# Second expert's first two token blocks interleaved, its weights decoded there instead of parked in DRAM

## Chip, core and metric

The kernel runs on one core of a Trainium2 chip. The metric is the device time of one execution in microseconds, as the median of several runs. TensorE does the matrix multiplications (PE, with PEld for its weight loads), VectorE (DVE), ScalarE (ACT) and GpSimd (POOL) the elementwise work, and SyncE's queue (SP) issues the transfers.

## What is computed

Three stages follow one another. A complex gated linear recurrence over 768 time steps for 4 batches of 8 heads of dimension 48 gives a matrix x of 3072 tokens by 384. Two feed-forward experts are applied to all tokens:

```
x  = attention(q, k, v, a_re, a_im)               # 3072 x 384
x1 = (sigmoid(x @ w_gate) * (x @ w_val)) @ w_out  # 384 -> 1536 -> 384
h  = x1 @ w2_in                                   # 384 -> 2048
out = (h * sigmoid(h)) @ w2_out                   # 2048 -> 384
```

The weights of the experts are held as float64 in DRAM.

## The kernel before

**Layout and stages.** Tokens are cut into 24 chunks of 128. The recurrence treats one chunk after another as a pipeline of small functions (s_load_a, s_nat1, s_den1, s_mix1 and so on); a list of "beats" says which function of which chunk is emitted when. The first expert treats nine blocks of chunks, three with two chunks and six with three (256 and 384 tokens). Each block has F1 = 12 steps, one for 128 hidden columns: 9 matmuls for the gate, 9 for the value, and 9 for the output of the step before. The recurrence's beats are spread among the steps of the blocks up to block 7. The second expert treats eight blocks (NB2) of 384 tokens in F2 = 16 steps each: 9 matmuls for h into ps_h, and 9 for the output of the step before into three accumulators acc.

**Split operands.** A product in full precision is three fast matmuls (mm3, L402 to L405): each operand is a high part and a remainder. The chain behind a step's matmuls in the second expert is: Tanh on ScalarE (L974), (tanh + 1) * h on VectorE into sg (L976), the high part hh on ScalarE (L980), the remainder hl on VectorE (L982). In the first expert the same four are L896, L899, L907, L909. TensorE needs hh and hl one step later.

**Weights.** A weight is one tile of 128 x 384 values. w_load (L326) brings its 64-bit words, 384 KB, by SP's queue. w_decode (L344) makes a float32 of them: L348 on ScalarE, L349 and L350 on VectorE, L351 on GpSimd. w_split (L354) makes the high part on ScalarE (L357) and the remainder (L358) on GpSimd and VectorE by turns. conv_to (L747) brings an expert's weights in order up to a given number; it loads up to four and decodes up to two weights ahead. The first expert's 36 weights stay in the 37 slots of the pool wpool, and each slot becomes free behind its last use in block 8. The pool w2p, with twelve slots, opens when the recurrence is over (close_att, L818).

**The second expert's 32 weights.** The first twelve (ND, direct=12) are decoded by conv_to (L926) in the first expert's last two blocks, once the recurrence's beats are out: from step 8 of block 7 on, the count of steps times rate2/10 = 1.8, at most 8 in block 7 (w2slots minus l2). The other twenty are *parked*: from block 2, step 6 on, every third step decodes and splits one weight (park, L371; its load by park_load, L365) and writes the result, 384 KB, to DRAM (w2_d, L378). The split there is L376 on ScalarE and L377 on VectorE. In block 8 unpark_to (L381) reads them back into freed slots of wpool (L385).

**Second expert.** Block by block, step by step (L959 to L993). The next block's input is loaded at step 2 (x1_load, L795) and split at step 13 (x1_split, L800: L803 on ScalarE, L804 on VectorE). Accumulators come from the pools pot and pacc by turns. finish2 (L947) writes a block's result. From block 1 on, check_to (L832) loads every one of the 68 weights again and checks its range (w_guard, L331: L338 on VectorE, L342 on ScalarE), eight weights in ten steps, tied behind the step's own instructions.

**What sets the order.** TensorE runs its instructions in program order (man=['PE']). The other engines' instructions and the transfers are put into order at build time by a scheduler that works with the program's order as priority and a model of the times. At run time each engine and each queue is strictly in order.

Of the kernel before, what the change touches and what calls it, by code (L numbers as in the profile page):

```python
# [9 lines left out]
F32 = mybir.dt.float32  # L10
F32R = mybir.dt.float32r
# [29 lines left out]
    gr=8,  # L41
# [36 lines left out]
    wrate=80,  # L78
    wlead=12,
    w2slots=12,  # L80
    rate2=18,
    c2a=16,
    rate3=20,
    park=30,
    direct=12,
    pacc=8,
    ve='GV',
    beats=8,
# [161 lines left out]
def tile_kernel(ctx, tc, q, k, v, a_re, a_im, w_gate, w_val, w_out, w2_in, w2_out, out):  # L250
# [93 lines left out]
    def w_decode(raw):  # L344
        lo, hi = raw[:, :, :, 0], raw[:, :, :, 1]
        two = wst.tile([128, 2, KD, 128], I32, tag="two", name="two")
        tmp, rnd = two[:, 0], two[:, 1]
        A.activation(rnd, lo.bitcast(U32), AF.Copy, scale=2.0 ** -29)  # L348
        V.tensor_scalar(tmp, hi, 3, 0x3FFFFFFF, ALU.logical_shift_left, ALU.bitwise_and)  # L349
        V.scalar_tensor_tensor(hi, hi, -0x40000000, tmp, ALU.bitwise_and, ALU.bitwise_or)  # L350
        G.tensor_tensor(hi, hi, rnd, ALU.add)  # L351
        return raw, two

    def w_split(pool, raw, nm, n):  # L354
# [2 lines left out]
        A.copy(t[:, 0], w)  # L357
        (V if CFG["ve"][n % len(CFG["ve"])] == "V" else G).tensor_tensor(t[:, 1], w, t[:, 0].bitcast(F32), ALU.subtract)  # L358
        return t

    w2_d = [dram.tile([128, 2, KD, 128], F32, name=f"w2_d{n}") for n in range(2 * F2)]
    ND = CFG["direct"]
    parked = [ND, None]

    def park_load():  # L365
        n = parked[0]
        raw = wst.tile([128, KD, 128, 2], I32, tag="two", name="raw2")
        src2(*order2[n])(raw)
        parked[1] = raw

    def park():  # L371
        n = parked[0]
        raw, two = w_decode(parked[1])
        w = raw[:, :, :, 1].bitcast(F32)
        two = two.bitcast(F32R)
        A.copy(two[:, 0], w)  # L376
        V.tensor_tensor(two[:, 1], w, two[:, 0].bitcast(F32), ALU.subtract)  # L377
        SP.dma_start(w2_d[n], two.bitcast(F32))  # L378
        parked[0] += 1

    def unpark_to(n):  # L381
        while unparked[0] < min(n, 2 * F2):
            i = unparked[0]
            t = wpool.tile([128, 2, KD, 128], F32R, tag="w", name="w2")
            SP.dma_start(t.bitcast(F32), w2_d[i])  # L385
            w2[order2[i]] = t
            unparked[0] += 1

    unparked = [ND]

    EA = 32
    EB = D - EA
# [402 lines left out]
    def x1_load(i):  # L795
        xs = w2p.tile([128, KD, BT2], F32, tag="xs", name="xs", bufs=3)
        SP.dma_start(xs, x1_d[:, :, i * BT2:(i + 1) * BT2].rearrange("k p t -> p k t"))
        return xs
# [13 lines left out]
    def src2(f, j):  # L812
        return (w_in_src(w2_in, f), w_out_src(w2_out, f))[j]
# [9 lines left out]
            pot = fast.enter_context(tc.tile_pool(name="pot", bufs=3, space=PSUM))  # L823

    w2p = pot = None
    c2f = psteps = 0
    conv2 = dict(ld=0, dec=0, sp=0)
    with tc.manual_schedule(engines={getattr(mybir.EngineType, e) for e in CFG["man"]}):
        checks = [src1(*o) for o in order1] + [src2(*o) for o in order2]
# [22 lines left out]
        for gi, group in enumerate(groups):  # L852
# [23 lines left out]
            for si, (i, f) in enumerate(steps):  # L876
                n = blocks[i] * C
                col = sum(blocks[b] for b in group if b < i) * C
                conv_to(conv1, order1, src1, pool1, w1, 3 * (f + 1))
                if f == 0:  # L880
                    beats_upto(0, beats_for(i))
                psg = pgv.tile([128, BT], F32, tag="g", name="ps_g")
                psv = pgv.tile([128, BT], F32, tag="v", name="ps_v")
                for ps, j in ((psg, 0), (psv, 1)):
                    for kk in range(KD):
                        if i == 0:
                            PE.matmul(ps[:, :n], word(f, j, kk), xT[i][0][:, kk, :n], start=kk == 0, stop=kk == KD - 1)
                            continue
                        w = w1[f, j]
                        xh, xl = xT[i]  # L890
                        mm3(ps[:, :n], w[:, 0, kk], w[:, 1, kk], xh[:, kk, :n], xl[:, kk, :n], kk == 0, kk == KD - 1)
                    if ps is psg:
                        sg = hp.tile([128, BT], F32, tag="sg", name="sg")
                        need(ATAN, SIN)
                        with crit():
                            lut(A.activation(sg[:, :n], psg[:, :n], AF.Tanh, scale=0.5))  # L896
                        beats_upto(2 * si + 1)
                with crit():
                    V.scalar_tensor_tensor(sg[:, :n], sg[:, :n], 1.0, psv[:, :n], ALU.add, ALU.mult)  # L899
                if prev is not None:  # L900
                    moe_out(*prev)
                if i == 0:
                    h = (sg,)
                else:
                    h = (hp.tile([128, BT], F32R, tag="hh", name="hh"), hp.tile([128, BT], F32R, tag="hl", name="hl"))
                    with crit():
                        A.copy(h[0][:, :n], sg[:, :n])  # L907
                    with crit():
                        V.tensor_tensor(h[1][:, :n], sg[:, :n], h[0][:, :n].bitcast(F32), ALU.subtract)  # L909
                if si == 0 and gi:  # L910
                    finish1(*fin)
                conv_to(conv1, order1, src1, pool1, w1, 3 * (f + 1) + CFG["wlead"])
                if 12 * i + f >= CFG["park"] and parked[0] < 2 * F2:
                    psteps += 1
                    if psteps % 3 == 0:
                        park()
                        if parked[0] < 2 * F2:
                            park_load()
                    elif psteps == 1:
                        park_load()  # L920
                if done == nbeats and i >= NB - 2:
                    assert parked[0] == 2 * F2
                    close_att()
                    c2f += 1
                    lim2 = len(order2) if i == NB - 1 else CFG["w2slots"] - CFG["l2"]
                    conv_to(conv2, order2[:ND], src2, pool2, w2, min(c2f * CFG["rate2"] // 10, lim2))  # L926
                    if i == NB - 1:
                        unpark_to(ND + 2 * (f - 1))
                beats_upto(2 * si + 2)
                if i == NB - 1 and f == 2:  # L930
                    raw_n = x1_load(0)
                if i == NB - 1 and f == 7:
                    nxt = x1_split(raw_n)
                prev = (f, h, [a[:, col:col + n] for a in acc], n,
                        si == 0, si == len(steps) - 1)
# [20 lines left out]

        NB2 = NT // BT2
        prev = None
        for i in range(NB2):  # L959
            cur = nxt  # L960
            acc = [(pacc if i % 2 else pot).tile([128, 512], F32, tag="acc", name="acc2") for _ in range(BT2 // 128)]
            for f in range(F2):
                conv_to(conv2, order2[:ND], src2, pool2, w2, ND)
                unpark_to(2 * (f + 1))
                if f == 2 and i + 1 < NB2:
                    raw_n = x1_load(i + 1)
                ps = pgv.tile([128, BT], F32, tag="gv"[f % 2], name="ps_h")
                w = w2[f, 0]
                for kk in range(KD):
                    mm3(ps[:, :BT2], w[:, 0, kk], w[:, 1, kk], cur[0][:, kk], cur[1][:, kk], kk == 0, kk == KD - 1)  # L970
                sg = hp.tile([128, BT], F32, tag="sg", name="sg2")
                need(ATAN, SIN)
                with crit():
                    lut(A.activation(sg[:, :BT2], ps[:, :BT2], AF.Tanh, scale=0.5))  # L974
                with crit():
                    V.scalar_tensor_tensor(sg[:, :BT2], sg[:, :BT2], 1.0, ps[:, :BT2], ALU.add, ALU.mult)  # L976
                hh = hp.tile([128, BT], F32R, tag="hh", name="hh2")
                hl = hp.tile([128, BT], F32R, tag="hl", name="hl2")
                with crit():
                    step["A"] = A.copy(hh[:, :BT2], sg[:, :BT2])  # L980
                with crit():
                    step["V"] = V.tensor_tensor(hl[:, :BT2], sg[:, :BT2], hh[:, :BT2].bitcast(F32), ALU.subtract)  # L982
                if prev is not None:
                    moe2_out(*prev)
                    if prev[0] == F2 - 1:
                        finish2(i - 1, prev[2])
                if f == F2 - 3 and i + 1 < NB2:
                    nxt = x1_split(raw_n)
                unpark_to(2 * F2)
                if i:  # L990
                    gs += 1
                    check_to(gs * CFG["gr"] // 10)
                prev = (f, (hh, hl), acc)  # L993
        assert checked == len(checks)
        moe2_out(*prev)
        finish2(NB2 - 1, prev[2])
    bad = lim[:, 4:8]
    good = const.tile([1, 1], I32, name="good")
    V.tensor_reduce(bad[:, 0:1], under, AX.X, ALU.add)
# [43 lines left out]
```

## Time and profile before

| | |
|---|---|
| median of 3 runs | 1155.65 us (1153.68 to 1159.09) |
| profiled execution, own time | 1156.26 us |
| its span, first to last instruction | 1154.5 us |
| TensorE (PE) busy in the span | 1070.1 us, 93% |
| VectorE (DVE) busy | 737.9 us, 64% |
| ScalarE (ACT) busy | 647.3 us, 56% |
| GpSimd (POOL) busy | 251.7 us, 22% |
| HBM read, written | 89.65 MB, 17.30 MB |

All times in the profile are microseconds from the span's start unless marked ns. A wait is put down to the instruction that released it. A group of instructions bears the line of the kernel (L349) that issued it; a helper's line stands for all its callers. A matmul's shown duration overlaps the next one's, so the distance of two starts is the better measure of what one takes. The granted clock of TensorE is 1.00 of full speed from 100 us on.

### The profile page before, as it was taken

How to read it: one execution, taken by the hardware profiler on the slowest of the kernel's cores; microseconds unless marked ns; L12 is line 12 of the kernel's file. 1: busy time of each engine (PE TensorE's matmuls, PEld its weight loads, DVE VectorE, ACT ScalarE, POOL GpSimd, SP SyncE). 2: the span in 40 equal slices, each digit the busy share in tenths (PEclk: the TensorE clock that was granted, in tenths of full speed). 3: DMA queues.
4: the chain of work that ended last, by engine and by line, in shares of the span. 5: the costliest groups of instructions: out<-in, count | busy, mean ns of one | idle time of the engine just before them, and what ended most of it. 6: DMA issues, size and time to landing. Idle time of an engine off the chain costs nothing.

```text
span 1154.5 us, 20813 instructions
## 1 busy us (share of the span) xinstructions
PE 1070.1 (93%) x7786; PEld 1036.1 (90%) x7786; DVE 737.9 (64%) x1336; ACT 647.3 (56%) x1270; POOL 251.7 (22%) x253
## 2 busy tenths in 40 slices
PE   0568989999999999999999999999999999999998
PEld 0457878999999999999999989999999999999997
DVE  7889987788777877776676393334454555545333
ACT  6685877778776666666663252234444454545332
POOL 6566653223333322222221060000000000000000
PEclk9978999999999999999999999999999999999999
DMA  9574445463555554423222349701343443400000
GB/s 241 125 222 131 119 101 152 122 157 94 134 128 129 142 130 115 93 63 83 63 50 66 95 136 302 244 1 55 104 137 96 151 137 96 130 1 21 1 22 23
DMA packets 222522, 127.33 MB, mean 110 GB/s; under 512 B 132944, under 2 KB 210128, under 8 KB 222416
## 3 DMA queue, kind: packets, MB, share of 16 engines
q1 hardware_dynamic: 222416, 125.94, 40.2%
q8 instruction: 63, 1.03, 0.4%
q14 instruction: 43, 0.35, 0.1%
HBM read 89.65 MB, written 17.30 MB: 93 GB/s over the span
## 4 chain that ended last, share of the span: by engine, by line
PE 61%; DVE 14%; DMA 9%; ACT 6%; issue 4%; SPq 4%; POOL 2%; DVEq 0%; POOLq 0%; ACTq 0%
PE acc L405 8%; PE acc L404 8%; PE acc L403 8%; PE ps_h L405 5%; PE ps_h L404 5%; PE ps_h L403 5%; PE ps_v L403 3%; PE ps_g L403 2%; PE ps_g L405 2%; PE ps_g L404 2%; PE ps_v L405 2%; PE ps_v L404 2%; PE ps_a L610 2%; DMA raw<-in_moe_w_out_dram 2%; DVE two L349 2%
## 5 line engine op out<-in xcount | busy, mean ns | idle before, releaser
L976 DVE SCALAR_TENSOR_TENSOR sg<-sg,ps_h 128x384 f32<-128x384 f32 x128 | 70.7, 553 | 133.3 <-ACT sg L974 133.3
L974 ACT ACTIVATE sg<-ps_h 128x384 f32<-128x384 f32 x128 | 62.9, 492 | 147.9 <-PE ps_h L405 147.9
L405 PE MATMUL acc<-w,hl 128*128 128x384 f32 x384 | 129.2, 336 | 2.7 <-DVE hl L982 2.5
L403 PE MATMUL acc<-w,hh 128*128 128x384 f32 x384 | 128.9, 336 | 0.4 <-ACT hh L980 0.2
L404 PE MATMUL acc<-w,hh 128*128 128x384 f32 x384 | 128.4, 334 | 0.0
L405 PE MATMUL ps_h<-xh,w 128*128 128x384 f32 x384 | 128.3, 334 | 0.0
L403 PE MATMUL ps_h<-xh,w 128*128 128x384 f32 x384 | 128.3, 334 | 0.0
L404 PE MATMUL ps_h<-xl,w 128*128 128x384 f32 x384 | 128.3, 334 | 0.0
L982 DVE TENSOR_TENSOR hl<-sg,hh 128x384 fp32r<-128x384 f32 x128 | 71.3, 557 | 66.7 <-ACT hh L980 66.7
L980 ACT CAST hh<-sg 128x384 fp32r<-128x384 f32 x128 | 65.8, 514 | 74.2 <-DVE sg L976 74.0
L403 PE MATMUL ps_v<-xh,w 128*128 128x384 f32 (+1 forms) x288 | 97.4, 338 | 6.6 <-DVE sg L899 6.6
L351 POOL TENSOR_TENSOR raw<-raw,two 128x384 int32<-128x384 int32 x68 | 77.5, 1140 | 118.2 <-DVE raw L350 47.4
L907 ACT CAST hh<-sg 128x384 fp32r<-128x384 f32 (+1 forms) x96 | 46.5, 484 | 100.7 <-DVE sg L899 100.7
L899 DVE SCALAR_TENSOR_TENSOR sg<-sg,ps_v 128x384 f32<-128x384 f32 (+1 forms) x108 | 54.0, 500 | 71.1 <-PE ps_v L405 70.4
L404 PE MATMUL acc<-hl,w 128*128 128x384 f32 (+1 forms) x288 | 94.2, 327 | 5.1 <-DVE hl L909 5.0
L403 PE MATMUL ps_g<-xh,w 128*128 128x384 f32 (+1 forms) x288 | 96.3, 334 | 1.5 <-ACT sg L896 1.5
L403 PE MATMUL acc<-hh,w 128*128 128x384 f32 (+1 forms) x288 | 92.8, 322 | 0.1
L405 PE MATMUL acc<-hh,w 128*128 128x384 f32 (+1 forms) x288 | 92.6, 322 | 0.0
L404 PE MATMUL ps_v<-xl,w 128*128 128x384 f32 (+1 forms) x288 | 92.6, 321 | 0.0
L405 PE MATMUL ps_g<-xh,w 128*128 128x384 f32 (+1 forms) x288 | 92.6, 321 | 0.0
L405 PE MATMUL ps_v<-xh,w 128*128 128x384 f32 (+1 forms) x288 | 92.5, 321 | 0.0
L404 PE MATMUL ps_g<-xl,w 128*128 128x384 f32 (+1 forms) x288 | 92.5, 321 | 0.0
(151 smaller groups left out, 2915.6 us busy)
## 6 DMA issues: line engine op xcount, KB each, us to landing
raw<-in_moe_w_out_dram SPq DMA_DIRECT2D x56, 384.0 KB, 3.8
raw<-in_moe_w_in_dram SPq DMA_DIRECT2D x32, 384.0 KB, 3.5
raw<-in_moe_w_gate_dram SPq DMA_DIRECT2D x24, 384.0 KB, 3.9
raw<-in_moe_w_val_dram SPq DMA_DIRECT2D x24, 384.0 KB, 4.1
w_d<-two SPq DMA_DIRECT2D x20, 384.0 KB, 3.7
w<-w_d SPq DMA_DIRECT2D x20, 384.0 KB, 4.4
kst<-kc SPq DMA_DIRECT2D x72, 64.5 KB, 2.7
kst<-r SPq DMA_DIRECT2D x72, 64.5 KB, 2.8
```

Of the source, the lines that this page charges most:

```text
L349: V.tensor_scalar(tmp, hi, 3, 0x3FFFFFFF, ALU.logical_shift_left, ALU.bitwise_and)
L351: G.tensor_tensor(hi, hi, rnd, ALU.add)
L403: PE.matmul(o, lhi, rhi, start=first, stop=False)
L404: PE.matmul(o, lhi, rlo, start=False, stop=False)
L405: PE.matmul(o, llo, rhi, start=False, stop=last)
L610: PE.matmul(ps[:, h, :], kst[:, g * hh + h, 1:CX], qst[:, g * hh + h, :], start=True, stop=True)
L899: V.scalar_tensor_tensor(sg[:, :n], sg[:, :n], 1.0, psv[:, :n], ALU.add, ALU.mult)
L907: A.copy(h[0][:, :n], sg[:, :n])
L974: lut(A.activation(sg[:, :BT2], ps[:, :BT2], AF.Tanh, scale=0.5))
L976: V.scalar_tensor_tensor(sg[:, :BT2], sg[:, :BT2], 1.0, ps[:, :BT2], ALU.add, ALU.mult)
L980: step["A"] = A.copy(hh[:, :BT2], sg[:, :BT2])
L982: step["V"] = V.tensor_tensor(hl[:, :BT2], sg[:, :BT2], hh[:, :BT2].bitcast(F32), ALU.subtract)
```

## The change

Parking is gone: w2_d, park_load, park and unpark_to, with their calls. All 32 weights of the second expert go through conv_to: rate2 falls from 18 to 12, so the 16 steps at the end of the first expert bring 19 of them, and the second expert's steps go on with one a step (c2a + n2, to 32 at the sixteenth step). The first two blocks of the second expert run together: steps of block 0 and block 1 alternate, block 1 two steps behind (lag=2), so that each weight is used by both blocks soon after it is decoded. Block 1's input is loaded at the first step and split ahead of block 1's first. The banks of ps_h alternate by the running number of the step. The checks begin with block 2.

```diff
@@ -78,11 +78,10 @@
     wrate=80,
     wlead=12,
     w2slots=12,
-    rate2=18,
+    rate2=12,
     c2a=16,
     rate3=20,
-    park=30,
-    direct=12,
+    lag=2,
     pacc=8,
     ve='GV',
     beats=8,
@@ -358,36 +357,6 @@
         (V if CFG["ve"][n % len(CFG["ve"])] == "V" else G).tensor_tensor(t[:, 1], w, t[:, 0].bitcast(F32), ALU.subtract)
         return t
 
-    w2_d = [dram.tile([128, 2, KD, 128], F32, name=f"w2_d{n}") for n in range(2 * F2)]
-    ND = CFG["direct"]
-    parked = [ND, None]
-
-    def park_load():
-        n = parked[0]
-        raw = wst.tile([128, KD, 128, 2], I32, tag="two", name="raw2")
-        src2(*order2[n])(raw)
-        parked[1] = raw
-
-    def park():
-        n = parked[0]
-        raw, two = w_decode(parked[1])
-        w = raw[:, :, :, 1].bitcast(F32)
-        two = two.bitcast(F32R)
-        A.copy(two[:, 0], w)
-        V.tensor_tensor(two[:, 1], w, two[:, 0].bitcast(F32), ALU.subtract)
-        SP.dma_start(w2_d[n], two.bitcast(F32))
-        parked[0] += 1
-
-    def unpark_to(n):
-        while unparked[0] < min(n, 2 * F2):
-            i = unparked[0]
-            t = wpool.tile([128, 2, KD, 128], F32R, tag="w", name="w2")
-            SP.dma_start(t.bitcast(F32), w2_d[i])
-            w2[order2[i]] = t
-            unparked[0] += 1
-
-    unparked = [ND]
-
     EA = 32
     EB = D - EA
 
@@ -823,7 +792,7 @@
             pot = fast.enter_context(tc.tile_pool(name="pot", bufs=3, space=PSUM))
 
     w2p = pot = None
-    c2f = psteps = 0
+    c2f = 0
     conv2 = dict(ld=0, dec=0, sp=0)
     with tc.manual_schedule(engines={getattr(mybir.EngineType, e) for e in CFG["man"]}):
         checks = [src1(*o) for o in order1] + [src2(*o) for o in order2]
@@ -910,22 +879,11 @@
                 if si == 0 and gi:
                     finish1(*fin)
                 conv_to(conv1, order1, src1, pool1, w1, 3 * (f + 1) + CFG["wlead"])
-                if 12 * i + f >= CFG["park"] and parked[0] < 2 * F2:
-                    psteps += 1
-                    if psteps % 3 == 0:
-                        park()
-                        if parked[0] < 2 * F2:
-                            park_load()
-                    elif psteps == 1:
-                        park_load()
                 if done == nbeats and i >= NB - 2:
-                    assert parked[0] == 2 * F2
                     close_att()
                     c2f += 1
                     lim2 = len(order2) if i == NB - 1 else CFG["w2slots"] - CFG["l2"]
-                    conv_to(conv2, order2[:ND], src2, pool2, w2, min(c2f * CFG["rate2"] // 10, lim2))
-                    if i == NB - 1:
-                        unpark_to(ND + 2 * (f - 1))
+                    conv_to(conv2, order2, src2, pool2, w2, min(c2f * CFG["rate2"] // 10, lim2))
                 beats_upto(2 * si + 2)
                 if i == NB - 1 and f == 2:
                     raw_n = x1_load(0)
@@ -956,44 +914,56 @@
 
         NB2 = NT // BT2
         prev = None
-        for i in range(NB2):
-            cur = nxt
-            acc = [(pacc if i % 2 else pot).tile([128, 512], F32, tag="acc", name="acc2") for _ in range(BT2 // 128)]
-            for f in range(F2):
-                conv_to(conv2, order2[:ND], src2, pool2, w2, ND)
-                unpark_to(2 * (f + 1))
-                if f == 2 and i + 1 < NB2:
-                    raw_n = x1_load(i + 1)
-                ps = pgv.tile([128, BT], F32, tag="gv"[f % 2], name="ps_h")
-                w = w2[f, 0]
-                for kk in range(KD):
-                    mm3(ps[:, :BT2], w[:, 0, kk], w[:, 1, kk], cur[0][:, kk], cur[1][:, kk], kk == 0, kk == KD - 1)
-                sg = hp.tile([128, BT], F32, tag="sg", name="sg2")
-                need(ATAN, SIN)
-                with crit():
-                    lut(A.activation(sg[:, :BT2], ps[:, :BT2], AF.Tanh, scale=0.5))
-                with crit():
-                    V.scalar_tensor_tensor(sg[:, :BT2], sg[:, :BT2], 1.0, ps[:, :BT2], ALU.add, ALU.mult)
-                hh = hp.tile([128, BT], F32R, tag="hh", name="hh2")
-                hl = hp.tile([128, BT], F32R, tag="hl", name="hl2")
-                with crit():
-                    step["A"] = A.copy(hh[:, :BT2], sg[:, :BT2])
-                with crit():
-                    step["V"] = V.tensor_tensor(hl[:, :BT2], sg[:, :BT2], hh[:, :BT2].bitcast(F32), ALU.subtract)
-                if prev is not None:
-                    moe2_out(*prev)
-                    if prev[0] == F2 - 1:
-                        finish2(i - 1, prev[2])
-                if f == F2 - 3 and i + 1 < NB2:
-                    nxt = x1_split(raw_n)
-                unpark_to(2 * F2)
-                if i:
-                    gs += 1
-                    check_to(gs * CFG["gr"] // 10)
-                prev = (f, (hh, hl), acc)
+        lag = CFG["lag"]
+        steps2 = []
+        for f in range(F2 + lag):
+            steps2 += [(0, f)] if f < F2 else []
+            steps2 += [(1, f - lag)] if f >= lag else []
+        steps2 += [(i, f) for i in range(2, NB2) for f in range(F2)]
+        xs_n, x2, accs = {}, {0: nxt}, {}
+        n2 = 0
+        for i, f in steps2:
+            n2 += 1
+            if f == 0:
+                accs[i] = [(pacc if i % 2 else pot).tile([128, 512], F32, tag="acc", name="acc2") for _ in range(BT2 // 128)]
+                if i == 0:
+                    xs_n[1] = x1_load(1)
+                elif i == 1:
+                    x2[1] = x1_split(xs_n.pop(1))
+            cur = x2[i]
+            conv_to(conv2, order2, src2, pool2, w2, 2 * (f + 1))
+            if f == 2 and i and i + 1 < NB2:
+                xs_n[i + 1] = x1_load(i + 1)
+            ps = pgv.tile([128, BT], F32, tag="gv"[n2 % 2], name="ps_h")
+            w = w2[f, 0]
+            for kk in range(KD):
+                mm3(ps[:, :BT2], w[:, 0, kk], w[:, 1, kk], cur[0][:, kk], cur[1][:, kk], kk == 0, kk == KD - 1)
+            sg = hp.tile([128, BT], F32, tag="sg", name="sg2")
+            need(ATAN, SIN)
+            with crit():
+                lut(A.activation(sg[:, :BT2], ps[:, :BT2], AF.Tanh, scale=0.5))
+            with crit():
+                V.scalar_tensor_tensor(sg[:, :BT2], sg[:, :BT2], 1.0, ps[:, :BT2], ALU.add, ALU.mult)
+            hh = hp.tile([128, BT], F32R, tag="hh", name="hh2")
+            hl = hp.tile([128, BT], F32R, tag="hl", name="hl2")
+            with crit():
+                step["A"] = A.copy(hh[:, :BT2], sg[:, :BT2])
+            with crit():
+                step["V"] = V.tensor_tensor(hl[:, :BT2], sg[:, :BT2], hh[:, :BT2].bitcast(F32), ALU.subtract)
+            if prev is not None:
+                moe2_out(prev[1], *prev[2:])
+                if prev[1] == F2 - 1:
+                    finish2(prev[0], prev[3])
+            if f == F2 - 3 and i and i + 1 < NB2:
+                x2[i + 1] = x1_split(xs_n.pop(i + 1))
+            conv_to(conv2, order2, src2, pool2, w2, max(2 * (f + 2), CFG["c2a"] + n2))
+            if i > 1:
+                gs += 1
+                check_to(gs * CFG["gr"] // 10)
+            prev = (i, f, (hh, hl), accs[i])
         assert checked == len(checks)
-        moe2_out(*prev)
-        finish2(NB2 - 1, prev[2])
+        moe2_out(*prev[1:])
+        finish2(NB2 - 1, prev[3])
     bad = lim[:, 4:8]
     good = const.tile([1, 1], I32, name="good")
     V.tensor_reduce(bad[:, 0:1], under, AX.X, ALU.add)
```

## Rows read from the trace of the kernel before

**Rows 1.** Busy time by stretch: stretch, its length, busy per engine (instructions), clock, DMA share, GB/s.
```profile
142.00:200.00 58.00, 52.13 (x464) 47.76 (x463) 46.58 (x81) 45.46 (x95) 26.99 (x26) 1.00 0.51 127
200.00:450.00 250.00, 242.32 (x2155) 234.61 (x2155) 197.22 (x384) 178.32 (x320) 74.39 (x73) 1.00 0.51 127
450.00:655.00 205.00, 204.61 (x1713) 201.01 (x1706) 134.19 (x255) 117.07 (x205) 40.81 (x42) 1.00 0.31 72
655.00:742.00 87.00, 83.42 (x524) 81.12 (x523) 45.74 (x69) 31.00 (x62) 20.58 (x18) 1.00 0.67 222
742.00:793.00 51.00, 50.79 (x291) 50.18 (x290) 18.81 (x34) 16.53 (x33) 0.00 (x0) 1.00 0.11 36
```
**Rows 2.** TensorE's waits, 200 to 450 us: total us, times, longest us.
```profile
PE ps_v L403 <- DVE sg L899: 4.9, 7, 1.2
PE acc L404 <- DVE hl L909: 2.6, 4, 1.2
```
**Rows 3.** Single lines: times, ns min/median/max, first and last start, shape.
```profile
L376 ACT CAST two<-raw x20: 516/543/582, 142.1 to 442.2; 128x384 fp32r<-128x384 f32 x20
...
L385 SPq DMA_DIRECT2D w<-w_d x20: 319/320/423, 691.5 to 714.9; - x20
...
L338 DVE TENSOR_REDUCE least<-raw x68: 543/544/547, 800.2 to 1063.2; 128x1 f32<-128x384 f32 x68
```
**Rows 4.** Instructions in order of time around 350 us: start, us, engine, line, operation.
```profile
344.50 1.35 POOL L351 TENSOR_TENSOR raw<-raw,two 128x384 int32<-128x384 int32 x1
...
345.35 0.92 DVE L582 SCALAR_TENSOR_TENSOR f<-f,p 128x384 f32<-128x384 f32 x1
...
348.32 0.54 DVE L377 TENSOR_TENSOR two<-raw,two 128x384 fp32r<-128x384 f32 x1
...
349.57 0.54 DVE L899 SCALAR_TENSOR_TENSOR sg<-sg,ps_v 128x384 f32<-128x384 f32 x1
...
348.67 0.34 PE L405 MATMUL ps_g<-xh,w 128*128 128x384 f32 x1
350.16 0.44 PE L403 MATMUL ps_v<-xh,w 128*128 128x384 f32 x1 [1.15 <-DVE sg L899]
```
**Rows 5.** The same view of VectorE ahead of 298.09 us.
```profile
297.15 0.55 DVE L673 TENSOR_TENSOR sd<-st,kst 96x384 f32<-96x384 f32 x1 [1.86 <-DMA kst<-r]
```
**Rows 6.** Lines of the decoding: times, ns min/median/max, first and last start, shape.
```profile
L349 DVE TENSOR_SCALAR two<-raw x68: 333/354/1193, 8.2 to 691.9; 128x384 int32<-128x384 int32 x68
...
L350 DVE SCALAR_TENSOR_TENSOR raw<-raw,two x68: 524/559/1378, 8.6 to 692.3; 128x384 int32<-128x384 int32 x68
...
L351 POOL TENSOR_TENSOR raw<-raw,two x68: 1007/1048/1499, 11.0 to 693.8; 128x384 int32<-128x384 int32 x68
...
L358 POOL TENSOR_TENSOR w<-raw,w x24: 1012/1157/1668, 59.1 to 692.2; 128x384 fp32r<-128x384 f32 x24
L358 DVE TENSOR_TENSOR w<-raw,w x24: 531/776/1376, 60.5 to 695.5; 128x384 fp32r<-128x384 f32 x24
```
**Rows 7.** TensorE's waits, 655 to 745 us.
```profile
PE ps_v L403 <- DVE sg L899: 1.7, 1, 1.7
PE acc L404 <- DVE hl L909: 1.4, 2, 1.0
```
**Rows 8.** VectorE and GpSimd in order of time, 673 to 675 us.
```profile
673.72 1.19 DVE L349 TENSOR_SCALAR two<-raw 128x384 int32<-128x384 int32 x1
...
673.47 1.23 POOL L351 TENSOR_TENSOR raw<-raw,two 128x384 int32<-128x384 int32 x1 [0.95 <-ACT w L357]
```
**Rows 9.** A step's chain in the second expert, 766 to 769 us.
```profile
766.23 0.55 DVE L976 SCALAR_TENSOR_TENSOR sg<-sg,ps_h 128x384 f32<-128x384 f32 x1 [1.43 <-ACT sg L974]
...
767.36 0.56 DVE L982 TENSOR_TENSOR hl<-sg,hh 128x384 fp32r<-128x384 f32 x1 [0.58 <-ACT hh L980]
...
768.91 0.33 PE L405 MATMUL acc<-w,hl 128*128 128x384 f32 x1
```

## The prediction, before the run

> **What bounds the kernel now.** I read the busy time by stretch first, then the waits of TensorE, then the order of VectorE's and GpSimd's instructions ahead of the longest waits. From 200 us on TensorE sets the time: it is busy 242.3 of 250 us between 200 and 450, 204.6 of 205 between 450 and 655, 83.4 of 87 around the start of the second expert, 50.8 of 51 in its first block [rows 1]. No other engine is nearly that full there, so the time can only fall where TensorE idles, and rises by whatever new idling it gets. The reader should see that 200 to 450 us idles 7.7 us and the next 205 us only 0.4, though the recurrence runs beside the first expert in both; parking runs from 142.1 to 442.2 us [rows 3] and is the plainest difference. The waits name the chain of the gate: in 200 to 450 TensorE waited seven times for sg (4.9 us) and four times for hl (2.6 us), both made by VectorE [rows 2].
>
> A stall costs more than its idle time. Around the one at 350.16 us the matmuls started at 348.67 and 350.16, 1.49 us apart [rows 4]; the regular distance is 50.79 us over 291 matmuls, 0.17 us [rows 1]. So 1.32 us were lost where the view shows 1.15. I add 0.17 us to each stall.
>
> **What is removed: 20 parkings and 20 reads.** One parking issues a load, six engine instructions (L348, L349, L350, L351, L376, L377) and a write on SP's queue; the way back issues a read. On VectorE that is 0.354 + 0.559 us [rows 6] and another subtraction, which took 0.54 at 348.32 [rows 4], so 1.46 us a weight; GpSimd gives 1.05 us [rows 6]. What it does to the chain shows at 350.16: VectorE has no idle time in the rows before, the parked weight's L377 stands in the queue ahead of sg's L899, and GpSimd's L351 delayed the recurrence's own instruction (L582, 0.92 us) in the same queue [rows 4]. Not every stall is of this kind: the longest wait for hl, 1.2 us [rows 2], came at 298.09 us, where VectorE itself had stood 1.86 us for a DMA of the recurrence and ran that one's instruction first [rows 5]; it stays.
>
> The sum for 200 to 450 us: 4.9 + 2.6 = 7.5 us in 11 stalls, plus 11 x 0.17 = 1.9, is 9.4. The rate of the stretch without parking, one stall of 0.4 us (0.57 with its surcharge) in 205 us, would leave 0.7: 8.7 us go at the most. I take off the stall that waits for a DMA, 1.2 + 0.17 = 1.4, and get **7.3 us gained**. The bounds are 0 (once VectorE is earlier, what is late next is the recurrence's chain: its DMA wait and its own VectorE work, which fills 197.2 of 250 us with the parkings' 17 x 1.46 = 25 us or so in it [rows 1]) and 10.7, with 2 us added for the three parkings or so before 200 us, where TensorE idles 5.9 of 58 us [rows 1] but mostly for the recurrence; my value leaves these at nothing. It lies near the upper end since the comparison stretch carries the same work.
>
> The 20 writes and the 20 reads themselves I cost at nothing: all went through SP's queue, the reads left at 691.5 to 714.9 us [rows 3], well ahead of their use from about 742 on, and TensorE's longest waits name none of them [rows 2, 7]. What covers them is that lead; they are gone, and the same number of raw loads takes their places in the queue. These wait for the same weight slots, and behind them stand the first expert's result writes and the second's input loads; if that lead were lost, the step whose weight is missing would wait for a load.
>
> **What is added late: 20 more decodings.** Before, 12 weights are decoded around 660 to 695 us, 18 to ten steps. After, the rate is 12 to ten: 16 steps (four of block 7, twelve of block 8) give 19 weights, 7 more than before, and the remaining 13 come one a step in the steps 4 to 16 of the second expert. Each costs VectorE 0.354 + 0.559 and, every second one, 0.776 us; GpSimd 1.05 and, every second one, 1.16 [rows 6]: 1.30 and 1.63 us a weight. A step of the second expert lasts 18 x 0.174 = 3.1 us, of which its chain takes 0.55 + 0.56 on VectorE [rows 9]. So VectorE is at 2.4 of 3.1 us, full but not over; no engine becomes the bound by its sum.
>
> What counts is the chain. In a quiet step hl is ready at 767.36 + 0.56 = 767.92, and its first matmul starts at 768.91 [rows 9]: 0.99 us of slack. The first weights' price is on show: they left 1.7 us for sg and 1.4 for hl, two stalls [rows 7], of which the longest hl wait, 1.0 us, lies at the change of expert, after the decoding. That leaves 2.1 us in two stalls, with surcharge 2.4 us over 12 weights, 0.20 a weight. The bounds for the 20 are 0 (VectorE is busy only 18.8 of 51 us in block 0 [rows 1], and the chain may fit between) and 0.8 each, 16 us (below). I take **0.15 a weight, 3.0 us lost**: the rate per step falls by a third in block 7 and 8, and the tighter step of the second expert gives part of that back.
>
> Here a mechanism is on show that speaks against the change. At 673.72 VectorE's L349 took 1.19 us instead of 0.354, since GpSimd had begun its 1.23 us addition at 673.47; it ended 0.2 us after GpSimd did [rows 8].  The Trainium skill, in "SBUF — State Buffer", section "SBUF: two separate sides", states the rule: GpSimd shares one port pair with VectorE's instructions that have two SBUF inputs or run in a two-port mode, an exclusive lock, and the later one waits out the whole instruction of the other. The trace agrees for L349; by the rule hl's subtraction, the last link of the chain with two SBUF inputs, is caught as well whenever an addition of GpSimd has begun. By the rows the late term is 3.0 us; by the rule, taken for every decoding, it would be the 16 of the rival "lock" below.
>
> **What moves at no cost.** Interleaving changes no matmul: a step still holds 9 of h and 9 of the step before. Block 1's input split moves from step 14 to step 4, before the first decoding; its VectorE part already ran ahead of the second expert in before, where it lies in the stall at the change of expert, and I leave that stall as it is. Both blocks' accumulators have their own banks. The weight checks start one block later; they end at 1063.2 us now [rows 3], and 16 steps of 3.1 us later is 1113, still 40 us before the end.
>
> **Sum.** 7.3 - 3.0 = 4.3 us of gain on the profiled execution's own time, 1156.26 us: 1152.0. That execution is 0.6 us above the median of the runs, 1155.65, so I forecast **1151.4 us**. Half a per cent, 5.8 us, is about what a measurement of this kernel can tell from no change: faster means below 1149.9, slower above 1161.4.
>
> **Rivals.**
> - *All returned, chance 0.20.* The parkings' stalls go with the early ones (10.7 us) and the late decodings hide in VectorE's free time: 1155.65 - 10.7 = 1145.0. For it: the clean stretch from 450 on. Against it: the 2.4 us that 12 decodings cost already.
> - *The stalls were not the parkings', chance 0.18.* VectorE's queue before a stall holds mostly the recurrence; another order leaves other stalls. If a quarter comes back, 1.8 us, and the late part costs 0.20 x 20 = 4.0: 1157.9, not to be told from no change.
> - *Lock, slower, chance 0.12.* In a step of the second expert a decoding's L349 or L350 that GpSimd has caught stands ahead of sg (0.84 us late by L349's 1.19 against 0.354), and hl is caught too, by as much again: 1.68 less 0.99 of slack is 0.69, with surcharge about 0.8 us a weight. Twenty are 16 us: 1155.65 + 16 - 7.3 = 1164.4. It decides from 7.3 / 20 = 0.37 us a weight, and shows as slower from 0.66.
> - *Not done as said, chance 0.06.* All engines but TensorE are ordered by a scheduler that moves work up as soon as its buffers are free; the reads left by 714.9 us [rows 3], while the program asks for the last of them in block 8's last steps, near 735. The decodings may all land in block 8, at a density like the first twelve's: 0.20 x 20 = 4.0 lost, 1152.4.
>
> The forecast has 0.44. Its own range is 1147 to 1156 (gain of 5 to 9, loss of 1 to 6, not both at their ends). About 0.16 of the 0.44 lies below 1149.9; with the first rival that is 0.36 for faster. Slower is the lock's 0.12 and 0.01 of the second rival. The rest, 0.51, is the same. The range reaches from just below the first rival's time to the second's upper side, 1144 to 1160, and leaves out the lock and the part of the first rival in which more than 10.7 us comes back.
>
> **What would show it.** Right: the stretch 200 to 440 us with four or fewer waits for sg and hl and under 3.5 us idle; two to five short stalls between 655 and 795 us beyond the one at the change of expert; GpSimd busy beyond 742 us, where it now has 0.00 [rows 1]; no wait of TensorE for a weight. The step on parking is wrong if the 200 to 440 stretch keeps more than 5 us of such waits; the step on decoding is wrong if the steps 4 to 16 of the second expert show a wait for hl in most steps (lock), or none at all (all returned). A wait for a raw load, or checks at the end of the trace, would refute what I costed at nothing.

## The result, and the profile after

The changed kernel takes 1169.04 us in the median (1165.99 to 1170.07, four runs) against 1155.44: ratio 1.0111, interval 1.0092 to 1.0129. It is 13.6 us slower where 4.3 us of gain were forecast, and lies outside the range. Its profiled execution has a span of 1167.5 us, 13.0 more than before.

Where it went is read off four starts of the Tanh, the first link of the chain: the first of block 0, that of block 7's step 5 (all of the recurrence's heavy part is behind it, and no late decoding has begun), the first and the last of the second expert. Timeline of ScalarE in the kernel before:

```profile
81.17 0.36 ACT L896 ACTIVATE sg<-ps_g 128x256 f32<-128x256 f32 x1
...
644.00 0.49 ACT L896 ACTIVATE sg<-ps_g 128x384 f32<-128x384 f32 x1 [2.01 <-PE ps_g L405]
...
744.68 0.49 ACT L974 ACTIVATE sg<-ps_h 128x384 f32<-128x384 f32 x1 [1.65 <-PE ps_h L405]
...
1145.36 0.49 ACT L974 ACTIVATE sg<-ps_h 128x384 f32<-128x384 f32 x1 [1.50 <-PE ps_h L405]
```

And after:

```profile
81.00 0.36 ACT L865 ACTIVATE sg<-ps_g 128x256 f32<-128x256 f32 x1
...
633.50 0.49 ACT L865 ACTIVATE sg<-ps_g 128x384 f32<-128x384 f32 x1 [2.01 <-PE ps_g L374]
...
752.82 0.49 ACT L944 ACTIVATE sg<-ps_h 128x384 f32<-128x384 f32 x1 [1.65 <-PE ps_h L374]
...
1156.78 0.49 ACT L944 ACTIVATE sg<-ps_h 128x384 f32<-128x384 f32 x1 [1.49 <-PE ps_h L374]
```

The *early stretch* (first to second row) falls from 562.8 to 552.5 us: 10.3 gained. The *late stretch* (second to third), from the end of the recurrence to the second expert, grows from 100.7 to 119.3: 18.6 lost, more than all of the gain. The second expert (third to fourth) grows from 400.7 to 404.0: 3.3 lost. The last 1.4 us lie at the two ends of the span.

Busy time by stretch after, to be held against [rows 1]:

```profile
200.00:450.00 250.00, 247.06 (x2239) 242.16 (x2238) 179.00 (x346) 167.49 (x293) 59.52 (x60) 1.00 0.37 80
...
650.00:697.00 47.00, 42.36 (x230) 39.19 (x228) 42.92 (x61) 25.26 (x52) 28.71 (x25) 1.00 0.60 200
697.00:736.00 39.00, 28.91 (x140) 27.18 (x140) 37.51 (x50) 20.12 (x42) 25.63 (x24) 0.91 0.45 142
...
750.00:800.00 50.00, 49.79 (x286) 49.18 (x285) 18.25 (x33) 16.10 (x33) 0.00 (x0) 1.00 0.08 26
```

TensorE's waits after, 200 to 450 us and then 650 to 745 us, to be held against [rows 2, 7]:

```profile
PE ps_v L372 <- DVE sg L868: 2.1, 2, 1.7
PE acc L373 <- DVE hl L878: 0.6, 1, 0.6
...
PE acc L373 <- DVE hl L878: 8.6, 7, 2.0
PE ps_v L372 <- DVE sg L868: 6.0, 5, 1.8
```

The early waits for sg and hl fell from 7.5 us to 2.7. In 697 to 736 us TensorE idles 10 of 39 us, VectorE is busy 37.5 of 39, and TensorE's granted clock is 0.91. From 750 us on GpSimd has nothing to do: no decoding lies in the second expert. The decoding's first VectorE instruction says so as a line (range of starts, before 8.2 to 691.9 [rows 6]):

```profile
L348 DVE TENSOR_SCALAR two<-raw x68: 336/379/1190, 8.2 to 730.5; 128x384 int32<-128x384 int32 x68
```

The last decoding begins at 730.5 us, though the program writes 13 of them into the second expert's steps. This is one step of block 8, from sg to the next sg, and how its wait of 2 us comes about, in order of time on VectorE, ScalarE, GpSimd and TensorE:

```profile
697.92 0.54 DVE L868 SCALAR_TENSOR_TENSOR sg<-sg,ps_v 128x384 f32<-128x384 f32 x1
698.39 0.70 DVE L348 TENSOR_SCALAR two<-raw 128x384 int32<-128x384 int32 x1
699.12 1.28 DVE L349 SCALAR_TENSOR_TENSOR raw<-raw,two 128x384 int32<-128x384 int32 x1
700.33 0.35 DVE L348 TENSOR_SCALAR two<-raw 128x384 int32<-128x384 int32 x1
700.71 1.35 DVE L349 SCALAR_TENSOR_TENSOR raw<-raw,two 128x384 int32<-128x384 int32 x1
701.99 0.55 DVE L878 TENSOR_TENSOR hl<-sg,hh 128x384 fp32r<-128x384 f32 x1
702.46 1.38 DVE L357 TENSOR_TENSOR w<-raw,w 128x384 fp32r<-128x384 f32 x1
703.76 1.18 DVE L348 TENSOR_SCALAR two<-raw 128x384 int32<-128x384 int32 x1
704.97 0.56 DVE L349 SCALAR_TENSOR_TENSOR raw<-raw,two 128x384 int32<-128x384 int32 x1
705.45 0.55 DVE L868 SCALAR_TENSOR_TENSOR sg<-sg,ps_v 128x384 f32<-128x384 f32 x1
...
698.50 0.51 ACT L876 CAST hh<-sg 128x384 fp32r<-128x384 f32 x1 [0.36 <-DVE sg L868]
...
697.76 1.11 POOL L350 TENSOR_TENSOR raw<-raw,two 128x384 int32<-128x384 int32 x1 [0.65 <-ACT w L356]
698.83 1.16 POOL L357 TENSOR_TENSOR w<-raw,w 128x384 fp32r<-128x384 f32 x1
700.64 1.01 POOL L350 TENSOR_TENSOR raw<-raw,two 128x384 int32<-128x384 int32 x1 [0.65 <-DVE raw L349]
...
700.21 0.34 PE L372 MATMUL acc<-hh,w 128*128 128x384 f32 x1
702.59 0.44 PE L373 MATMUL acc<-hl,w 128*128 128x384 f32 x1 [2.04 <-DVE hl L878]
```

hh was ready at 699.01, but between sg and hl stand four instructions of two decodings. Three of them began while GpSimd was in an addition or a remainder and took 0.70, 1.28 and 1.35 us instead of 0.35, 0.56 and 0.56 [rows 6]: 1.86 us too long together, about the 2.04 that TensorE waited.

A third thing shows when the whole step is read: three decodings stand in it, VectorE has no idle time, and from sg to sg it takes 7.53 us, where TensorE's 27 matmuls need 4.68, the distance in the undisturbed steps of the run spread below. From 683 to 728 us six steps are like this, three decodings and 6.9 to 7.9 us each; a seventh has two and takes 5.3. These seven steps are 17 us too long, nearly the whole late loss, and VectorE, not TensorE, sets their pace. By the undisturbed durations of [rows 6, 9] an average step of three decodings would take VectorE 3 x (0.35 + 0.56) + 1.5 x 0.53 + 2 x 0.55, an estimate of 4.6 us: it would just fit.

So three things meet: the *order* (decodings ahead of hl), the *number* (three in a step) and the *hold-up* by GpSimd. The runs take the hold-up apart from the other two, and order and number only in part.

### The profile page after: what moved, and what is told of

It is laid out like the page before. It is cut to its first block, busy times and chain, and to the rows that moved or that the text cites. A ratio compares the mean times of both kernels' runs of the same rounds, so it can differ in the third digit from the quotient of the medians.

```text
span 1167.5 us, 20777 instructions
## 1 busy us (share of the span) xinstructions
PE 1073.6 (92%) x7786; PEld 1039.6 (89%) x7786; DVE 748.8 (64%) x1326; ACT 648.8 (56%) x1270; POOL 262.2 (22%) x263
## 4 chain that ended last, share of the span: by engine, by line
PE 69%; DVE 13%; DMA 5%; issue 5%; ACT 4%; SPq 2%; POOL 1%; DVEq 0%; POOLq 0%; ACTq 0%
PE acc L374 8%; PE acc L373 8%; PE acc L372 8%; PE ps_h L374 5%; PE ps_h L372 5%; PE ps_h L373 5%; PE ps_v L372 3%; PE ps_g L372 3%; PE ps_g L374 3%; PE ps_y L633 3%; PE ps_g L373 3%; PE ps_v L374 3%; PE ps_v L373 3%; PE ps_a L579 3%; DVE two L348 3%
```

## Experiments

The comparisons name the late stretch, measured as above, 100.7 us before and 119.3 after, and the whole time's ratio to the kernel before. Theory: the loss comes from the order, since the scheduler brought the decodings forward into block 8. Rivals: the hold-up by GpSimd wherever a decoding stands; the interleaving itself; VectorE's sheer load. The expectations put the loss in block 8 at 22 us, which is about the 18.6 us of the late stretch and the second expert's 3.3 together.

**spread: late decodings tied behind the step's chain.** `after` puts an instruction behind a given one on its own engine.

```diff
-        A.activation(rnd, lo.bitcast(U32), AF.Copy, scale=2.0 ** -29)
-        V.tensor_scalar(tmp, hi, 3, 0x3FFFFFFF, ALU.logical_shift_left, ALU.bitwise_and)
+        tied("A", A.activation(rnd, lo.bitcast(U32), AF.Copy, scale=2.0 ** -29))
+        tied("V", V.tensor_scalar(tmp, hi, 3, 0x3FFFFFFF, ALU.logical_shift_left, ALU.bitwise_and))
...
+                    if i >= NB - 2:
+                        step["A"], step["V"] = step_a, step_v
```

(tied calls `after` once a step is known; the split's copy and VectorE's remainders are tied likewise.)

> The changed kernel with one difference: each late decoding and split is ordered behind the chain of the step in which the program writes it, so the scheduler can't bring it forward into block 8. Crowding theory (the loss comes from 24 decodings packed into block 8 at more than two a step): the decodings now stand at 1.2 and then one a step, TensorE's idle time between 650 and 800 us falls from 16 to at most 6 us, and the time is 1148 to 1155 us, not slower than before. Lock theory (each decoding costs what GpSimd's share of the port pair costs, wherever it stands): 32 decodings at 0.6 to 0.8 us, 1162 us or more.

1147.7 us, ratio 0.9929 (0.9905 to 0.9954): faster than both kernels, and just below the range given. TensorE idles 2.0 us between 640 and 800 us. Its late stretch:

```profile
632.85 0.49 ACT L873 ACTIVATE sg<-ps_g 128x384 f32<-128x384 f32 x1 [2.01 <-PE ps_g L382]
...
732.16 0.49 ACT L954 ACTIVATE sg<-ps_h 128x384 f32<-128x384 f32 x1 [2.97 <-PE ps_h L382]
```

The decoding's line in it:

```profile
L353 DVE TENSOR_SCALAR two<-raw x68: 333/353/1185, 8.2 to 777.2; 128x384 int32<-128x384 int32 x68
```

The late stretch is 99.3 us, 20.0 less than in the changed kernel, with decodings up to 777.2. A decoding at 1 a step behind the chain costs next to nothing, GpSimd's part included; "wherever it stands" falls. The tie changes order and number at once: each step now holds one or two decodings, not three, and lasts 4.68 us, so this run does not say which of the two did it.

**twelve: no late decoding of the other twenty.** This kernel leaves out twenty weights, so it does not compute the experts; it measures time alone.

```diff
-                    conv_to(conv2, order2, src2, pool2, w2, min(c2f * CFG["rate2"] // 10, lim2))
+                    conv_to(conv2, order2[:12], src2, pool2, w2, min(c2f * CFG["rate2"] // 10, lim2))
...
+            for n in range(12, 2 * F2):
+                w2[order2[n]] = w2[order2[n % 12]]
```

> The changed kernel without 20 of its late decodings: only the first twelve weights of the second expert are loaded and decoded, and they are used again in place of the other twenty. It measures what parking cost and what the interleaved loop costs by itself. If parking cost 10.5 us (the lead that the changed kernel has at block 7) and interleaving costs nothing: 1143 to 1147 us. If interleaving costs something of its own (the longer stall near 1063 us): 1148 to 1152 us. If the early lead is lost again anyway: 1155 us.

1147.17 us, 0.9919 (0.9891 to 0.9946), at the upper edge of the first case. The late stretch is 734.56 - 633.80 = 100.8 us:

```profile
633.80 0.49 ACT L865 ACTIVATE sg<-ps_g 128x384 f32<-128x384 f32 x1 [2.01 <-PE ps_g L374]
...
734.56 0.49 ACT L946 ACTIVATE sg<-ps_h 128x384 f32<-128x384 f32 x1 [1.65 <-PE ps_h L374]
```

So the twenty decodings, with their loads, make the whole of the late loss, 18.5 us, and without them the early gain stays. That gain is parking's: the early stretch is 561.8 to 563.3 us in the three runs that park and 551.9 to 555.8 in the eight that don't. The twelve decodings left here stand in six steps, two a step on the average, not tied and held up by GpSimd as before; the late stretch is only 1.5 us above that of spread. Decodings ahead of hl under the hold-up need not cost much, then, as long as they are few.

**parked_inter: interleaving alone**, the second expert's loop of the changed kernel in the kernel before, parking and reads kept.

```diff
+            conv_to(conv2, order2[:ND], src2, pool2, w2, ND)
+            unpark_to(2 * (f + 1))
...
+            unpark_to(2 * F2)
```

> The kernel before, parking and all, with the second expert's loop of the changed kernel alone (blocks 0 and 1 interleaved, checks from block 2 on). If interleaving is free: 1154 to 1157 us. If the order of the checks brings the stall near 1063 us and TensorE's lower clock behind it: 1158 to 1160 us, with the extra time after 1050 us.

1156.26 us, 1.0001 (0.9984 to 1.0018). With parking kept, interleaving is free within 0.2%, and so is the later start of the checks.

**nopool: late decodings without GpSimd**, in the changed kernel, nothing tied.

```diff
-                decs[cv["dec"]] = w_decode(raws.pop(cv["dec"]))[0]
+                decs[cv["dec"]] = w_decode(raws.pop(cv["dec"]), V if store is w2 else G)[0]
...
+                store[order[cv["sp"]]] = w_split(pool(cv["sp"]), decs.pop(cv["sp"]), "w", cv["sp"], "V")
```

> The changed kernel with the late decodings' GpSimd work on VectorE (L350's addition and every remainder). VectorE's sum for a weight is then 0.35 + 0.56 + 0.56 + 0.55 = 2.0 us, and 2.1 us was measured in the changed kernel with GpSimd's share caught in it. Crowding theory (VectorE's full queue is what stalls TensorE): 1164 to 1172 us, VectorE still busy over 90% in block 8. Lock theory (the caught instructions stall it): hl back at 0.56 us, at least half of the 22 us lost in block 8 returns, 1159 us or less.

1150.12 us, 0.9944 (0.9923 to 0.9965); the crowding theory, as I put it, missed by 14 us. Its late stretch:

```profile
634.73 0.49 ACT L865 ACTIVATE sg<-ps_g 128x384 f32<-128x384 f32 x1 [2.01 <-PE ps_g L374]
...
734.70 0.49 ACT L944 ACTIVATE sg<-ps_h 128x384 f32<-128x384 f32 x1 [1.65 <-PE ps_h L374]
```

Busy time in the same 39 us as above:

```profile
697.00:736.00 39.00, 36.96 (x212) 36.23 (x210) 34.22 (x76) 21.69 (x46) 0.00 (x0) 1.00 0.67 212
```

Two of VectorE's groups in them (count, busy us, mean ns, idle before):

```profile
L349 DVE SCALAR_TENSOR_TENSOR raw<-raw,two 128x384 int32<-128x384 int32 x14 | 7.7, 550 | 0.0
...
L348 DVE TENSOR_SCALAR two<-raw 128x384 int32<-128x384 int32 x13 | 4.4, 351 | 0.0
```

The decodings still crowd block 8 (13 begin in these 39 us, 14 in the changed kernel) and VectorE is busy 34.2 of 39 us, yet the late stretch is 100.0 us, TensorE is busy 37 of 39, and L349 and L348 are back at 550 and 351 ns. VectorE does more work here, 76 instructions against 50, and does it in time: what fills its queue in the changed kernel is the hold-up. The order alone is not the cause either: from 686 to 727 us five or six instructions of decodings stand between sg and hl in every step, where the changed kernel's long steps have two to four. What differs besides the hold-up is the number in a step: two decodings, not three, as the scheduler ordered the work anew.

**tied20: behind the chain, but two a step.** spread with rate2 = 20.

> The kernel of the run spread (late decodings tied behind their step's chain), with rate2 = 20 instead of 12: two decodings a step, so all 32 lie in blocks 7 and 8, nearly as dense as in the changed kernel (2.1 a step there), with GpSimd's part. Order theory (the harm is that decodings stand ahead of the chain in VectorE's queue, by a model of the times that does not count what GpSimd holds up): the chain comes first in each step here, so block 8 loses at most 5 us, 1146 to 1152 us. Density theory (two decodings a step with GpSimd's part don't fit, whatever their order): block 8 loses 15 us or more, 1160 us or more.

1159.33 us, 1.0013 (0.9999 to 1.0028): above the one range and just below the other, so neither theory is borne out. The late stretch is 743.53 - 635.25 = 108.3 us:

```profile
635.25 0.49 ACT L873 ACTIVATE sg<-ps_g 128x384 f32<-128x384 f32 x1 [2.01 <-PE ps_g L382]
...
743.53 0.49 ACT L954 ACTIVATE sg<-ps_h 128x384 f32<-128x384 f32 x1 [1.26 <-PE ps_h L382]
```

The largest wait of TensorE from 640 to 760 us is not in the steps but one for hh of 3.6 us, at the change of expert:

```profile
PE acc L380 <- ACT hh L884: 4.0, 2, 3.6
```

11.0 of the 18.6 us come back, but a step holds two decodings here, three in the changed kernel's long steps, so order and number share them. What stays, 7.6 us, is no price of density as such. Ten steps from 683.60 to 734.48 us take 5.09 us each instead of 4.68, 4 us in all, and the trace shows how:

```profile
703.93 0.54 DVE L876 SCALAR_TENSOR_TENSOR sg<-sg,ps_v 128x384 f32<-128x384 f32 x1
705.51 0.80 DVE L363 TENSOR_TENSOR w<-raw,w 128x384 fp32r<-128x384 f32 x1 [1.03 <-ACT w L361]
706.24 0.55 DVE L886 TENSOR_TENSOR hl<-sg,hh 128x384 fp32r<-128x384 f32 x1
```

A remainder (L363) that is tied behind one step's chain stands ahead of the next step's hl. It waits for ScalarE's copy (L361), which stands ahead of hh and has itself waited 2.41 us for GpSimd's addition. The tie keeps a decoding behind its own step's chain, not out of the next one's. At the change of expert hh stands behind such a copy and behind the split of the second expert's input, which is not tied.

**half_pool: only the additions moved to VectorE**, half of nopool's diff.

> The changed kernel, untied, with the late additions (L350) on VectorE and only every second remainder still on GpSimd: 0.6 us of GpSimd a weight instead of 1.6, VectorE's sum nearly as in nopool. If the loss in block 8 goes with GpSimd's part: between nopool (4 us lost there) and the changed kernel (22), about 10, 1153 to 1159 us. If any part of GpSimd does the full harm: 1165 us or more.

1155.21 us, 0.9988 (0.9975 to 1.0001). The late stretch is 102.9 us, nearer to nopool's 100.0 than the middle that I expected; the rest of the difference of the two runs lies in the early stretch (555.8 against 554.0) and in the second expert (406.3 against 402.4), read from a profiled execution of 1157.77 us, the slowest of its ten.

```profile
636.57 0.49 ACT L865 ACTIVATE sg<-ps_g 128x384 f32<-128x384 f32 x1 [2.01 <-PE ps_g L374]
...
739.43 0.49 ACT L944 ACTIVATE sg<-ps_h 128x384 f32<-128x384 f32 x1 [1.65 <-PE ps_h L374]
```

**rate18: the changed kernel with rate2 = 18.**

> The changed kernel with rate2 = 18, the value before. If the place of the decodings is set by free buffers and not by the step at which the program writes them, nothing moves: 1165 to 1173 us. If the written rate matters, decodings come earlier in program order than more of the chain and block 8 stalls more: 1174 us or more.

1171.13 us, 1.0106 (1.008 to 1.0132), late stretch 754.00 - 633.10 = 120.9 us. The written rate does nothing as long as the decodings aren't tied: three stand in the same six steps as at 12. That free buffers place them fits this, but is not shown.

**park_v: the parked weights' addition on VectorE**, in the kernel before.

```diff
-        raw, two = w_decode(parked[1])
+        raw, two = w_decode(parked[1], V)
```

> The kernel before, with the addition of the parked weights (L351) on VectorE instead of GpSimd; parking, reads and late decodings as before. If parking cost its 10 us through GpSimd's part (instructions caught, order set by a model that does not count it): most of it returns, 1147 to 1150 us. If it cost them by VectorE's time: VectorE has 0.56 us more a weight, 1155 to 1160 us.

1159.57 us, 1.002 (1.0008 to 1.0032). The early stretch does not shrink:

```profile
80.91 0.36 ACT L896 ACTIVATE sg<-ps_g 128x256 f32<-128x256 f32 x1
...
644.20 0.49 ACT L896 ACTIVATE sg<-ps_g 128x384 f32<-128x384 f32 x1 [2.01 <-PE ps_g L405]
```

563.3 us against 562.8. With 0.56 us more on VectorE in place of GpSimd's addition the early loss to parking stays the same. What share GpSimd's hold-up has in it stays open.

**spread_x1: the input splits tied as well**, on top of spread.

```diff
-        A.copy(xh, xs)
-        V.tensor_tensor(xl, xs, xh.bitcast(F32), ALU.subtract)
+        tied("A", A.copy(xh, xs))
+        tied("V", V.tensor_tensor(xl, xs, xh.bitcast(F32), ALU.subtract))
```

> The kernel of the run spread, in which also the splits of the second expert's input (L772, L773 of the changed kernel: 1.15 us on ScalarE, 1.36 us on VectorE) are ordered behind the chain of the step in which the program writes them. In spread they were brought forward into the chain at the change of expert and at block changes, where hl and hh were waited for 5.7 us in all. If order ahead of the chain is the cause there as well: these waits fall to 2 us or less, 1141 to 1145 us. If the input's transfer is late anyway and holds the step's chain: 1147 us or more.

1142.59 us, 0.9878 (0.9861 to 0.9894), the fastest of all. TensorE's waits from 640 us to the end:

```profile
PE ps_h L380 <- ACT xh L780: 1.3, 1, 1.3
PE ps_h L381 <- DVE xl L781: 1.0, 1, 1.0
PE acc L381 <- DVE hl L886: 0.4, 1, 0.4
```

2.7 us are left of spread's 5.7, where at most 2 were expected; the time is in the range. The waits at the later block changes, 3.8 us in spread, are gone. This is the one run in which order alone changes, and it shows that order costs by itself. What remains in the first two rows is block 1's first step, near 738 us, which waits for its own input's split, written just ahead of it.

## Why the prediction was wrong

**The parkings' term was too small.** 7.3 us were forecast and 10.3 measured, within the upper bound of 10.7; twelve shows that it stays. For its own stretch the term was right: of the first expert's lead 7.1 us arise between 202 and 457 us. Another 3.2 stand at 202 us already, which the forecast left at nothing and bounded by 2; TensorE's busy time from 142 to 200 us rose from 52.1 to 54.4. One part of the reason stays open: the step held GpSimd's L351 to be part of the harm, and park_v, which takes it off GpSimd for 0.56 us more on VectorE, gains nothing.

**The step that failed is "what is added late".** It put 7 of the 20 decodings into block 8 and 13 one a step into the second expert, because the program writes them so, and priced them at 0.15 us. Their place was wrong: all stood in blocks 7 and 8 and were over by 736 us. That is the rival "not done as said", which got 0.06; the prediction had the evidence for it, the reads that ran ahead of their place in the program, and did not carry it into its sum. The price was wrong too, and that rival's with it: 0.20 us a weight, taken from twelve weights, was multiplied as if it did not depend on how densely they stand. Measured, the twenty cost 18.6 us, 0.93 each. "No engine becomes the bound by its sum" failed with it: at three a step and held up, VectorE is busy 47.5 of the 48 us from 685 to 733 and stretches the steps to 7.5 us. The rival "lock" had nearly the right size (0.8) and the right hold-up, but put it into the second expert at one a step, where spread shows that it costs next to nothing.

**The mechanism on show was the right one.** The rule cited from the Trainium skill, "SBUF — State Buffer", section "SBUF: two separate sides", agrees with this trace: 0.70, 1.28 and 1.35 us for 0.35, 0.56 and 0.56 under GpSimd's instructions, and 351 and 550 ns where GpSimd is idle. As the prediction said, hl is caught as well: up to 1.37 us in the changed kernel, at most 0.56 in nopool. sg, which reads one operand from PSUM, kept 0.54 to 0.56 us in the late stretch of the changed kernel.

What the prediction missed is that the hold-up's price goes with the number of decodings in a step. twelve and spread keep the hold-up and lose next to nothing, at two a step and at one; nopool keeps the crowd and the order in block 8 and loses nothing, as none is held up; three a step under the hold-up cost 18.6 us. How much of this is order, and how much number, is not shown: no run has three a step behind the chain. Why the scheduler puts three decodings into a step was not looked into; that its model of the times lacks the hold-up fits the estimate of 4.6 us above, but is argued, not shown.

**What was costed at nothing.** Interleaving and the later checks: right where parking is kept (parked_inter); the checks now end 43 us before the end, 40 were forecast. Writes and reads: TensorE waits for no weight, but VectorE waited three times for a raw load between 676 and 685 us, 2.8 us in all, which the prediction had named as a sign against it; the longest, 1.22 us, stood ahead of an hl for which TensorE waited 0.64. The stall at the change of expert stayed at 1.0 us, as said.

The second expert's 3.3 us were not foreseen. The split of an input (L772) waited 2.2 us for its transfer near 1061 us and stood ahead of hh, as such splits already did before in smaller size; TensorE waited 1.2 us for that hh. The second expert's waits for hh are 1.3 to 3.0 us in the seven runs that neither park nor tie the splits, and at most 0.2 in the three that park, so they seem to belong to the change. Why the transfers come later was not looked into.

## What to carry to other kernels

Work that fills gaps belongs, by an explicit order, behind the chain that the bottleneck engine waits for; a place in the program is no place in the queue when a scheduler moves work up. The rate counts as much as the order: a piece tied behind one step's chain can stand ahead of the next one's. A price per piece read at one density is no price at another: count the pieces of a step, take each as long as it is under the other engine's hold-up, and see whether that sum still fits the step. With the ties and the rate of spread_x1, the change that lost 13.6 us gains 14.1.

## What was not expected of the hardware

TensorE's granted clock fell twice in block 8. TensorE had waited 0.6 to 2.0 us six times between 683 and 703 us; then its matmuls, which had started 0.17 us apart, started 0.32 us apart, as at the lower of its two levels (1.2 instead of 2.4 GHz), until 707.4 us:

```profile
703.57 0.35 PE L372 MATMUL acc<-hh,w 128*128 128x384 f32 x1
...
704.21 0.52 PE L372 MATMUL ps_g<-xh,w 128*128 128x384 f32 x1
704.53 0.52 PE L373 MATMUL ps_g<-xl,w 128*128 128x384 f32 x1
```

Behind two more waits, of 1.4 and 2.1 us, the same came from 718.0 to 720.9 us. The mean of 0.91 over 39 us corresponds to some 7 us at half speed. Here they need not have cost anything: VectorE, busy 47.5 of the 48 us from 685 to 733, set the pace, so that slower matmuls took the place of waiting; this is argued from the trace, no run shows it. Where TensorE sets the pace they did cost: behind the waits of 1.2 and 0.8 us at 1063 us ten matmuls started 0.32 us apart (granted clock 0.82 from 1066 to 1075 us), 1.5 us more and near half of the second expert's 3.3. A stall on TensorE can cost more than its idle time, by the matmuls after it.
